# Sliding-window attention: for one head of four, the mask of the transposed scores is added by VectorE in PSUM instead of by a TensorE product

## The chip, the cores and the metric

One core of a Trainium2 chip runs the whole kernel. The metric is the device time of one execution in microseconds (us). A core has TensorE (PE; its weight loads are listed as PEld), VectorE (DVE), ScalarE (ACT), GpSimd (POOL) and SyncE (SP, which here only issues transfers). The engines run side by side, each through its own queue in order, and wait for each other by semaphores.

## The reference

The kernel computes a block with conditioning, sliding-window attention and an MLP over 2048 rows of 576 values, in float32. The change lies in attention alone:

```python
B, S, D = x.shape
H = 32; Dh = D // H; W = 256
q, k, v = ...                          # from x @ wqkv, 32 heads of 18
scores = jnp.einsum("bhqd,bhkd->bhqk", q, k) * (Dh ** -0.5)
idx = jnp.arange(S)
mask = (idx[:, None] - idx[None, :] >= 0) & (idx[:, None] - idx[None, :] < W)
scores = jnp.where(mask[None, None], scores, -1e9)
p = _softmax(scores, axis=-1)
o = jnp.einsum("bhqk,bhkd->bhqd", p, v)
```

Around it: a layer norm with scale and shift from a condition vector, the projection to q, k and v before, the output projection `wo` after, then a shifted token-mixing MLP (w1, w2) and a large channel MLP (w3, w4).

## The kernel before

The program has three phases. Phase A makes layer norm, q, k and v, attention and the output projection; phase B the token-mixing MLP; phase C the channel MLP. Each phase lists its steps with a time written by hand, and plays them in the order of these times. In phase A the queues of PE, GpSimd and SP follow that order as it is written; for DVE and ACT a scheduler sets the order from its own estimates of readiness.

Attention goes in 32 units. A unit is four heads (chunk `c` of 8 heads, half `hq`) and one group `g` of 512 query rows, in the order c, g, hq. Each unit passes two stages:

- `s2`, the row maxima. For 4 query blocks and 4 heads, PE writes scores `sc` (queries on partitions, up to 384 keys) to one of three PSUM banks (L477), and DVE adds a mask and takes the maximum of each row in one instruction (L484, with a short read of its accumulator). The negative maxima (`mr`, L490 and L491) are transposed on PE (`mT`), copied by ACT (`ms`) and written by a transfer into two rows of the unit's operand `U`, so that the second stage's product subtracts the maximum by itself.
- `s3`, the probabilities. For each key-block position `b` (order 0, 3, 1, 2; the first row group has no 0) and each head `q` from 0 to 3, PE writes a transposed score block `X` (keys on partitions, 384 columns of queries) to one of three PSUM banks (L526: one product for b = 1 and 2, two for 0 and 3), adds the mask with a product of an identity matrix and a bfloat16 mask over the 256 columns at both ends (L527), and ACT takes the exponential into `P` (L533). After the blocks 0 and 3, and again after 1 and 2, PE multiplies `P` with V (`av`, L548): for each head its own 32 columns of the array. ACT copies `av` out (L553), PE transposes it (`oT`), and DVE divides by the sums (L562, L566).

`s3` of one unit is woven with `s2` of the one or two units that follow it: on PE a product `sc` and a block `X` alternate. The eight PSUM banks are three for `sc`, three for `X`, one for transposes and one for `av`. A block `X` can only be written when the exponential three blocks earlier has freed its bank; an `sc` only when the maximum three earlier has.

Of the kernel before, what the change touches and what calls it, by code (L numbers as in the profile page):

```python
# [12 lines left out]
ALU = mybir.AluOpType  # L13
# [6 lines left out]
P = 128  # L20
# [30 lines left out]
class Kern:  # L51
# [75 lines left out]
    def phase_a(self):  # L127
        nc = self.nc
# [10 lines left out]
        with ExitStack() as st:  # L139
# [301 lines left out]
            def unit(c, g, hq):  # L441
                return units[(2 * g + hq) % 4]
# [62 lines left out]
            def s3(c, g, hq):  # L505
                QZ, KZ = unit(c, g, hq)
                Pb, Xb, abox = {}, {}, []
                banks = [0, 3, 1, 2] if g else [3, 1, 2]

                def sc(b, q):  # L510
                    def f():
                        if q == 0:
                            Pb[b] = pp.tile([P, 4, 3 * P], F32, tag="P", name=f"P{c}_{g}_{hq}_{b}", bufs=self.b_p)
                        j = q // 2
                        X = self.ps.tile([P, 3, P], F32, tag="st", name=f"X{c}_{g}_{hq}_{b}_{q}", bufs=self.b_st)
                        if b == 0:
                            mms = [(0, 1, 0, 0), (1, 2, 1, 0)]
                            mk = maskb[:, 1, :].unsqueeze(1).to_broadcast([P, 2, P])
                        elif b < 3:
                            mms = [(0, 3, b + 1, b - 1)]  # L520
                            mk = maskb
                        else:
                            mms = [(0, 2, 4, 2), (2, 1, 5, 3)]
                            mk = maskb[:, 0, :].unsqueeze(1).to_broadcast([P, 2, P])
                        for n, (x0, nb, kb, qb) in enumerate(mms):
                            nc.tensor.matmul(X[:, x0:x0 + nb, :].rearrange("p a b -> p (a b)"), KZ[:, j, kb * P:(kb + 1) * P], QZ[:, q, qb * P:(qb + nb) * P], start=(n == 0), stop=False)  # L526
                        nc.tensor.matmul(X[:, 0::2, :], self.identb, mk, start=False, stop=True)  # L527
                        Xb[b, q] = X
                    return f

                def expo(b, q):
                    def f():
                        nc.scalar.activation(Pb[b][:, q, :], Xb[b, q].rearrange("p a b -> p (a b)"), AF.Exp, scale=SCALE)  # L533
                    return f

                def av(b):
                    def f():
                        if not abox:
                            abox.append(self.ps.tile([P, 512], F32, tag="av", name=f"av{c}_{g}_{hq}", bufs=self.b_av))
                        first = b == banks[0]  # L540
                        segs = {0: [(-1, 0, 2 * P, P), (-2, 0, P, 0)],
                                1: [(0, 0, 3 * P, 0)] if g else [(0, 0, 2 * P, 0), (0, 2 * P, P, 2 * P)],
                                2: [(1, P, 3 * P, 0)],
                                3: [(2, 2 * P, 2 * P, 0), (3, 3 * P, P, 2 * P)]}[b]
                        for n, (kb, q0, w, p0) in enumerate(segs):
                            for q in range(4):
                                hv = (8 * c + 4 * hq + q) * VA
                                nc.tensor.matmul(abox[0][32 * q:32 * q + 32, q0:q0 + w], V[4 * g + kb][:, hv:hv + 32], Pb[b][:, q, p0:p0 + w], start=(first and n == 0), stop=(b == banks[-1]))  # L548
                    return f

                def fin1():
                    avs = pp.tile([P, 512], F32, tag="avs", name=f"avs{c}_{g}_{hq}", bufs=1)
                    nc.scalar.copy(avs, abox[0])  # L553
                    abox.append(avs)

                def fin2():
                    avs = abox[1]
                    pt = self.ps.tile([P, 4, 4, 32], F32, tag="tr", name=f"oT{c}_{g}_{hq}", bufs=1)
                    for i in range(4):
                        nc.tensor.transpose(pt[:, i].rearrange("p a b -> p (a b)"), avs[:, i * P:(i + 1) * P], self.ident)  # L560
                    rc = sm.tile([P, 4, 4], F32, tag="rc", name=f"rc{c}_{g}_{hq}", bufs=2)
                    nc.vector.reciprocal(rc, pt[:, :, :, DH])  # L562
                    if hq == 0:
                        orow[c, g] = pp.tile([P, 4, 144], F32, tag="o", name=f"o{c}_{g}", bufs=self.b_o)
                    o = orow[c, g]
                    nc.vector.tensor_tensor(out=o[:, :, hq * 72:hq * 72 + 72].rearrange("p t (h d) -> p t h d", d=DH), in0=pt[:, :, :, 0:DH], in1=rc.unsqueeze(3).to_broadcast([P, 4, 4, DH]), op=ALU.mult)  # L566

                def fin3():
                    if hq == 1:
                        nc.sync.dma_start(self.od[g].rearrange("(t p) d -> p t d", p=P)[:, :, c * 144:(c + 1) * 144], orow[c, g])  # L570

                steps = []
                n = 0
                for k, b in enumerate(banks):
                    for q in range(4):
                        steps += [(n, sc(b, q)), (n + self.l_e, expo(b, q))]
                        n += 1
                    if (len(banks) - k) % 2:
                        for b2 in banks[max(0, k - 1):k + 1]:
                            steps.append((n + self.l_av + (1 if k < len(banks) - 1 else 0), av(b2)))  # L580
                return steps, n, fin1, fin2, fin3
# [118 lines left out]
            for c in range(NCH):  # L700
                for g in range(NGA):
                    for hq in range(2):
                        tb = 2 * u + hq + shift
                        n = 2 * u + hq
# [480 lines left out]
    c_w, c_t = 8.1, 8.6  # L1185
    lt, l_e, l_av, l_f, l_o = 1.2, 0.1, 0.0, 0.1, 0.12
    l_m = 0.1
    m_s4 = "v"
    m_eng = "vv" + "m" * 14
    n_warm = (16,)  # L1190
# [31 lines left out]
```

## Time and profile before

| | |
|---|---|
| median of 3 runs (lowest to highest) | 1789.46 us (1785.65 to 1795.23) |
| the profiled execution: time | 1788.75 us |
| the profiled execution: span in the trace | 1786.9 us |
| PE busy, share of the span | 97% |
| DVE busy | 55% |
| ACT busy | 33% |
| GpSimd busy | 22% |

In the profile a group of instructions reads: line, engine, operation, output<-inputs, shape, count | busy us in all, mean ns of one | idle time of the engine just before them, and what ended it. Rows of the timeline read: start in us from the span's start, duration in us, engine, line, operation, with neighbours of one kind merged ("x4") and, in brackets, the engine's idle time before it and what ended that. Rows of waits read: who <- whom, us in total, times, the longest. A stretch of the span reads: its bounds, its length, then for PE, PEld, DVE, ACT and POOL the busy us and count, then the granted clock of TensorE, the share of the transfer engines and GB/s. The ends of matmuls are modelled in the trace, so neighbouring matmuls can overlap in the rows; starts are the surer numbers.

Attention's maxima begin at about 196 us and its last exponentials are at 657 us. Before lie the projections, from 660 to about 860 us phase B, then phase C to the end.

### The profile page before, as it was taken

The page shows a single profiled execution, that of the slowest core. Times are in us where ns is not written, and L with a number is a line of the kernel's source. Part 1 is how long each engine was busy: PE and PEld are TensorE (multiplying, and loading weights), DVE is VectorE, ACT ScalarE, POOL GpSimd, SP SyncE. Part 2 cuts the span into 40 slices and gives each one's busy share as a digit, 9 for nine tenths or more (in the row PEclk, how much of TensorE's full clock was granted, in tenths as well). Part 3 has the DMA queues.
Part 4 walks back from the last instruction along what each step waited for, and adds up shares of the span by engine and source line. Part 5 has one row for each costly group of instructions (what it writes and reads, how often), then busy time and mean ns, then how long its engine had stood idle before and what let it go on. Part 6 is the DMA issues. An engine that isn't in the chain of part 4 may idle for free.

```text
span 1786.9 us, 30143 instructions
## 1 busy us (share of the span) xinstructions
PE 1731.2 (97%) x11700; PEld 1501.8 (84%) x11700; DVE 977.6 (55%) x2674; ACT 594.5 (33%) x1262; POOL 390.1 (22%) x379
## 2 busy tenths in 40 slices
PE   7999999999998988999899999999999999999999
PEld 5898767677767768899799999999999999999998
DVE  5402387778777875877544444444444444444434
ACT  4622166666664444354211111111111111111111
POOL 5511102222030110201432333234421121122100
PEclk8999999999999997999999999999999999999999
DMA  6434544544444556632211111111110000000002
GB/s 178 122 101 155 181 124 134 136 118 140 119 139 126 172 176 190 202 101 78 86 48 35 42 55 40 36 49 55 55 35 16 29 26 16 29 29 29 1 1 106
DMA packets 97712, 156.88 MB, mean 88 GB/s; under 512 B 11035, under 2 KB 40479, under 8 KB 97571
## 3 DMA queue, kind: packets, MB, share of 16 engines
q1 hardware_dynamic: 86612, 135.12, 25.5%
q10 hardware_dynamic: 10958, 19.85, 3.1%
q8 instruction: 92, 1.51, 0.4%
q14 instruction: 50, 0.40, 0.1%
HBM read 107.06 MB, written 47.20 MB: 86 GB/s over the span
## 4 chain that ended last, share of the span: by engine, by line
PE 55%; DVE 2%; POOL 0%; issue 0%; DMA 0%; ACT 0%; SPq 0%; POOLq 0%; ACTq 0%; DVEq 0%
PE p L1147 26%; PE p L1118 22%; PE p L1120 2%; PE p L1119 2%; PE w L1012 2%; PE pg L959 2%; DVE x L1013 0%; DMA r<-in_B_w_dram 0%; DVE G L977 0%; POOL CW L1102 0%; DVE LNT L70 0%; DVE CW L1097 0%; DVE xm L886 0%; DVE G L964 0%; DVE Gc L1129 0%
## 5 line engine op out<-in xcount | busy, mean ns | idle before, releaser
L1147 PEld LDWEIGHTS p<-CW,Gc 128*128 128x128 f32 x3456 | 473.8, 188 | 16.2 <-DVE Gc L1129 3.7
L1147 PE MATMUL p<-CW,Gc 128*128 128x288 f32 x3456 | 482.0, 295 | 3.5 <-DVE Gc L1129 3.5
L1118 PE MATMUL p<-LNT,CW 128*128 128x512 f32 x1728 | 419.1, 391 | 0.0
L1118 PEld LDWEIGHTS p<-LNT,CW 128*128 128x128 f32 x1728 | 316.2, 188 | 58.8
L1126 ACT ACTIVATE gfc<-p 128x512 f32<-128x512 f32 x144 | 86.2, 599 | 735.5 <-PE p L1120 735.5
L1151 DVE TENSOR_TENSOR acc<-p,acc 128x288 f32<-128x288 f32 x340 | 153.8, 455 | 319.2 <-PE p L1147 315.9
L484 DVE CUSTOM_DVE_ANT_0 sc<-sc,mask 128x384 f32<-128x384 f32 (+2 forms) x512 | 261.8, 555 | 84.1 <-PE sc L477 81.3
L533 ACT ACTIVATE P<-X 128x384 f32<-128x384 f32 x480 | 221.8, 490 | 107.9 <-PE X L527 94.5
L477 PE MATMUL sc<-U 126*128 126x384 f32 (+2 forms) x512 | 197.8, 404 | 5.5 <-DVE m L484 3.9
L526 PE MATMUL X<-U 128*128 128x384 f32 (+2 forms) x704 | 181.9, 317 | 4.8 <-DMA U<-ms 1.9
L1151 DVE TENSOR_TENSOR accw<-p,accw 128x288 f32<-128x288 f32 x204 | 90.0, 453 | 129.5 <-PE p L1147 128.1
L526 PEld LDWEIGHTS X<-U 128*128 128x128 f32 x704 | 126.7, 191 | 35.3 <-issue 23.9
L527 PE MATMUL X<-maskb,identb 128*128 128x256 bf16 x480 | 136.1, 284 | 0.0
L1129 DVE TENSOR_TENSOR Gc<-gfc,Gc 128x512 fp32r<-128x512 f32 x144 | 124.8, 867 | 4.5
L422 PE MATMUL pq<-hT,Wq 128*128 128x512 f32 x504 | 122.0, 400 | 2.3 <-POOL Wq L380 1.6
L422 PEld LDWEIGHTS pq<-hT,Wq 128*128 128x128 f32 x504 | 95.0, 190 | 24.8 <-POOL Wq L380 1.9
L477 PEld LDWEIGHTS sc<-U 126*128 126x128 f32 x512 | 98.5, 197 | 13.4 <-DVE m L484 9.6
L1098 POOL TENSOR_TENSOR CW<-r,CW 128x1024 fp32r<-128x1024 f32 x17 | 41.5, 2440 | 283.2 <-DVE CW L1096 283.2
L548 PE MATMUL av<-P,V 128*32 128x256 f32 (+2 forms) x1472 | 91.0, 379 | 0.0
L1128 ACT CAST Gc<-gfc 128x512 fp32r<-128x512 f32 x144 | 89.4, 621 | 4.6
L1102 POOL TENSOR_TENSOR CW<-r,CW 128x1152 fp32r<-128x1152 f32 x17 | 46.4, 2728 | 158.3 <-DVE CW L1101 158.3
L527 PEld LDWEIGHTS <-identb 128*128 128x128 bf16 x480 | 46.0, 96 | 36.0 <-issue 18.6
(1056 smaller groups left out, 1973.5 us busy)
## 6 DMA issues: line engine op xcount, KB each, us to landing
U<-qkh SPq DMA_DIRECT2D x156, 72.0 KB
U<-qkh SPq DMA_DIRECT2D x96, 108.0 KB
r<-in_B_w_dram SPq DMA_DIRECT2D x18, 576.0 KB
qkh<-hl ACTq DMA_DIRECT2D x36, 256.0 KB
qkl<-hl ACTq DMA_DIRECT2D x36, 256.0 KB
r<-in_B_w_dram SPq DMA_DIRECT2D x18, 512.0 KB
U<-qkl SPq DMA_DIRECT2D x78, 72.0 KB
U<-qkl SPq DMA_DIRECT2D x48, 108.0 KB
```

Source lines behind the costliest of these rows:

```text
L422: nc.tensor.matmul(pq, a, b, start=(n == 0), stop=(n == len(pl) - 1))
L477: nc.tensor.matmul(sc[:, lo:], QZ[:KR, q, i * P:(i + 1) * P], KZ[:KR, j, i * P + lo:(i + 3) * P], start=True, stop=True)
L484: nc.vector.tensor_tensor_reduce(out=sc[:, lo:], in0=sc[:, lo:], in1=mask[:, lo:], scale=1.0, scalar=-3e38, op0=ALU.add, op1=ALU.max, accu ...
L526: nc.tensor.matmul(X[:, x0:x0 + nb, :].rearrange("p a b -> p (a b)"), KZ[:, j, kb * P:(kb + 1) * P], QZ[:, q, qb * P:(qb + nb) * P], start ...
L527: nc.tensor.matmul(X[:, 0::2, :], self.identb, mk, start=False, stop=True)
L533: nc.scalar.activation(Pb[b][:, q, :], Xb[b, q].rearrange("p a b -> p (a b)"), AF.Exp, scale=SCALE)
L548: nc.tensor.matmul(abox[0][32 * q:32 * q + 32, q0:q0 + w], V[4 * g + kb][:, hv:hv + 32], Pb[b][:, q, p0:p0 + w], start=(first and n == 0), ...
L1118: nc.tensor.matmul(pg, W3[:, ws, fs], L[:, xs, :], start=(i == 0), stop=False)
L1128: nc.scalar.copy(Gh, gf)
L1129: nc.vector.tensor_tensor(out=Gl, in0=gf, in1=Gh.bitcast(F32), op=ALU.subtract)
L1147: nc.tensor.matmul(po, a, w, start=(i == 0), stop=(i == len(seq) - 1))
L1151: nc.vector.tensor_tensor(out=acc[t][:, cs], in0=po, in1=acc[t][:, cs], op=ALU.add)
```

## The change

For head q = 3 of each four, the product that adds the mask is left out, the last product of the scores closes the accumulation, and DVE adds the same bfloat16 mask to the 256 end columns of `X` in place in PSUM. Each unit has 3 or 4 such blocks (b values), 120 in all. Heads 0 to 2 keep the mask product.

```diff
                         for n, (x0, nb, kb, qb) in enumerate(mms):
-                            nc.tensor.matmul(X[:, x0:x0 + nb, :].rearrange("p a b -> p (a b)"), KZ[:, j, kb * P:(kb + 1) * P], QZ[:, q, qb * P:(qb + nb) * P], start=(n == 0), stop=False)
-                        nc.tensor.matmul(X[:, 0::2, :], self.identb, mk, start=False, stop=True)
+                            nc.tensor.matmul(X[:, x0:x0 + nb, :].rearrange("p a b -> p (a b)"), KZ[:, j, kb * P:(kb + 1) * P], QZ[:, q, qb * P:(qb + nb) * P], start=(n == 0), stop=(q in self.q_dve and n == len(mms) - 1))
+                        if q in self.q_dve:
+                            nc.vector.tensor_tensor(out=X[:, 0::2, :], in0=X[:, 0::2, :], in1=mk, op=ALU.add)
+                        else:
+                            nc.tensor.matmul(X[:, 0::2, :], self.identb, mk, start=False, stop=True)
                         Xb[b, q] = X
...
     l_m = 0.1
+    q_dve = (3,)
     m_s4 = "v"
```

The added lines move those behind by three: ACT's exponential is L536 in the changed kernel, `av` L551, the copy of `av` L556; the mask product is L530 and the add L528.

PE's order in attention is the same but for the products that are gone, and those of GpSimd and SP are the same there. The places of the adds on DVE are the scheduler's. In the rows below the numbers of a name are group, half, block or query block, and head, then a running number. First DVE's queue in the block that ends unit (c=1, g=1, hq=1): the add of b = 1, head 3, while the maxima are already those of unit (g=2, hq=1).

```order
 L484 ISA sc_2_1_0_3_4267,m_2_1_4220<-sc_2_1_0_3_4267,mask 128x384
 L484 ISA m_2_1_4220 128x1
+L528 TENSOR_TENSOR X_1_1_1_3_4269<-X_1_1_1_3_4269,maskb 128x2x128
 L484 ISA sc_2_1_1_0_4274,m_2_1_4220<-sc_2_1_1_0_4274,mask 128x384
 L484 ISA m_2_1_4220 128x1
```

The add stands behind the maximum of the second query block of this stretch, and four maxima (heads 0 to 3 of query block 1) follow. Then, on the same queue, the add of b = 2, head 3, the unit's last block:

```order
 L484 ISA sc_2_1_1_3_4298,m_2_1_4220<-sc_2_1_1_3_4298,mask 128x384
 L484 ISA m_2_1_4220 128x1
+L528 TENSOR_TENSOR X_1_1_2_3_4301<-X_1_1_2_3_4301,maskb 128x2x128
 L484 ISA sc_2_1_2_0_4305,m_2_1_4220<-sc_2_1_2_0_4305,mask 128x384
 L484 ISA m_2_1_4220 128x1
```

It stands behind those four maxima and ahead of one more. PE goes on to `av` right after writing this block and the scores of that last maximum. On ACT, at the blocks 0 and 3 of the next unit (g=2, hq=0), the order was

```order
L533 ACTIVATE P_2_0_3_4373<-X_2_0_3_0_4374 128x384
L533 ACTIVATE P_2_0_3_4373<-X_2_0_3_1_4383 128x384
L533 ACTIVATE P_2_0_3_4373<-X_2_0_3_2_4392 128x384
L533 ACTIVATE P_2_0_3_4373<-X_2_0_3_3_4400 128x384
L533 ACTIVATE P_2_0_1_4406<-X_2_0_1_0_4407 128x384
```

and in the changed kernel, at the same place on ACT, it is

```order
L536 ACTIVATE P_2_0_3_4373<-X_2_0_3_0_4374 128x384
L536 ACTIVATE P_2_0_3_4373<-X_2_0_3_1_4383 128x384
L536 ACTIVATE P_2_0_3_4373<-X_2_0_3_2_4392 128x384
L536 ACTIVATE P_2_0_1_4406<-X_2_0_1_0_4407 128x384
L536 ACTIVATE P_2_0_3_4373<-X_2_0_3_3_4400 128x384
```

The exponential of block 3, head 3, has moved behind that of block 1, head 0. On DVE the add of that block 3, head 3, stands behind the last maximum of unit (g=2, hq=1) and just ahead of the two steps that make the negative maxima:

```order
 L484 ISA sc_2_1_3_3_4397,m_2_1_4220<-sc_2_1_3_3_4397,mask 128x384
 L484 ISA m_2_1_4220 128x1
+L528 TENSOR_TENSOR X_2_0_3_3_4400<-X_2_0_3_3_4400,maskb 128x2x128
 L490 TENSOR_SCALAR mr_2_1_4414<-m_2_1_4220 128x4x4
 L491 SCALAR_TENSOR_TENSOR mr_2_1_4414<-m_2_1_4220,mr_2_1_4414 128x4x4
```

Nothing else there has changed its place on DVE, except that the division (L566) can swap with a neighbouring maximum.

## The prediction

> **What bounds the kernel now.** I read the page's engine totals, then the busy time by stage, then the groups by line and shape, then the waits, and last the timeline of one attention unit.
>
> ```profile
> span 1786.9 us, 30143 instructions
> PE 1731.2 (97%) x11700; PEld 1501.8 (84%) x11700; DVE 977.6 (55%) x2674; ACT 594.5 (33%) x1262; POOL 390.1 (22%) x379
> ...
> 240.00:600.00 360.00, 346.65 (x3124) 255.84 (x3124) 281.19 (x1054) 221.38 (x484) 59.80 (x63) 1.00 0.47 132
> ```
>
> TensorE (PE) is the bound overall. The last row is the stretch in which nearly all of the changed work lies; after its length come PE, weight loads, VectorE (DVE), ScalarE (ACT), GpSimd. PE is busy 346.65 of 360 us (96%), DVE 281.19 (78%). So PE bounds this stage too, but DVE is a good second here, not the idle 55% of the page.
>
> ```profile
> L484 DVE CUSTOM_DVE_ANT_0 sc<-sc,mask 128x384 f32<-128x384 f32 x448 | 239.4, 581 | 60.1 <-PE sc L477 58.1
> L533 ACT ACTIVATE P<-X 128x384 f32<-128x384 f32 x480 | 221.8, 490 | 107.9 <-PE X L527 94.5 <-PE sc L477 7.8 <-DMA qkh<-hl 2.3
> L1151 DVE TENSOR_TENSOR acc<-p,acc 128x288 f32<-128x288 f32 x340 | 153.8, 455 | 319.2 <-PE p L1147 315.9
> L527 PE MATMUL X<-maskb,identb 128*128 128x256 bf16 x480 | 136.1, 284 | 0.0
> ...
> ACT P L533 <- PE X L527: 94.5, 113, 2.7
> ...
> PEld sc L477 <- DVE m L484: 9.6, 21, 1.3
> ```
>
> DVE's main work is the row maximum of the scores (L484); PE hardly waits for it (9.6 us in all), and ACT waits for PE. The 480 mask products (L527) are what the change touches: 120 of them, head q=3 of each four.
>
> **One unit.** X is a block of transposed scores, named b (key block) and q (head). The rows below are the part b1q3 to b2q3 of one unit, the products with V (`av`) that end it, and the start of the next.
>
> ```profile
> 360.23 0.44 PE L526 MATMUL X<-U 128*128 128x384 f32 x1
> ...
> 361.57 0.34 PE L526 MATMUL X<-U 128*128 128x384 f32 x1
> ...
> 361.75 0.28 PE L527 MATMUL X<-maskb,identb 128*128 128x256 bf16 x1
> 361.77 0.57 DVE L484 CUSTOM_DVE_ANT_0 sc<-sc,mask 128x384 f32<-128x384 f32 x1
> 361.79 0.42 PE L477 MATMUL sc<-U 126*128 126x384 f32 x1
> 362.05 0.34 PE L526 MATMUL X<-U 128*128 128x384 f32 x1
> 362.16 0.48 ACT L533 ACTIVATE P<-X 128x384 f32<-128x384 f32 x1
> ...
> 362.25 0.60 DVE L484 CUSTOM_DVE_ANT_0 sc<-sc,mask 128x384 f32<-128x384 f32 x1
> ...
> 362.77 0.60 DVE L484 CUSTOM_DVE_ANT_0 sc<-sc,mask 128x384 f32<-128x384 f32 x1
> 362.95 1.64 ACT L533 ACTIVATE P<-X 128x384 f32<-128x384 f32 x4 [0.32 <-PE sc L477]
> ...
> 363.29 0.60 DVE L484 CUSTOM_DVE_ANT_0 sc<-sc,mask 128x384 f32<-128x384 f32 x1
> 363.50 0.43 PE L526 MATMUL X<-U 128*128 128x384 f32 x1
> ...
> 363.80 0.60 DVE L484 CUSTOM_DVE_ANT_0 sc<-sc,mask 128x384 f32<-128x384 f32 x1
> ...
> 364.16 1.50 PE L548 MATMUL av<-P,V 128*32 128x384 f32 x16
> 364.31 0.60 DVE L484 CUSTOM_DVE_ANT_0 sc<-sc,mask 128x384 f32<-128x384 f32 x1
> ...
> 365.59 0.49 PE L526 MATMUL X<-U 128*128 128x128 f32 x2
> 365.80 0.59 ACT L553 COPY avs<-av 128x512 f32<-128x512 f32 x1 [1.22 <-PE av L548]
> ...
> 366.42 0.57 DVE L484 CUSTOM_DVE_ANT_0 sc<-sc,mask 128x384 f32<-128x384 f32 x1 [1.45 <-PE sc L477]
> ```
>
> DVE runs the maxima back to back, one every 0.515 us (362.77, 363.29, 363.80, 364.31), and only rests 1.45 us while PE does `av`. ACT finishes the last exponential of the unit at 362.95+1.64 = 364.59, inside the `av` that began at 364.16, so PE never waits for it.
>
> **What is removed.** From X b1q3 (361.57) to the next X (362.05) PE takes 0.48 us for 384+256+384 = 1024 columns, so a mask product of 256 columns is worth 0.48*256/1024 = 0.12 us. As a lower end stands the 0.04 us from its start to that of the next product (361.75 to 361.79). 120 of them give 4.8 to 14.4 us of PE. I take 0.12, since PE streams without gaps here. Their weight loads lie beside other products and count nothing.
>
> **What is added.** 120 adds of 128x256 on DVE. The nearest row is L1151, an add with a PSUM operand, 128x288 in 0.455 us; by its elements 0.404. I take 0.42 from start to end. For how long an add holds the next instruction off, two adds of that size and their successor stand here:
>
> ```profile
> 849.74 0.81 DVE L1013 TENSOR_TENSOR x<-w,x 128x288 f32<-128x288 f32 x2
> ...
> 850.47 0.45 DVE L85 BATCH_NORM_STATS2 d13st<-x 128x6 f32<-128x288 f32 x1
> ```
>
> (850.47-849.74)/2 = 0.365 us for 288 elements; I take 0.35 for 256. That is 42 us of DVE in all, on an engine with 360-281 = 79 us free in this stage. By capacity it fits; by place it may not, because DVE's free time lies behind the maxima, and the add of the block's last head stands behind them too.
>
> **The end of the first block.** By DVE's order the add of b1q3 stands behind the maximum that starts at 361.77, and four maxima stand between it and the add of b2q3. The first add takes the slot of 362.25 and passes DVE on at 362.60. Four maxima of 0.515 follow, to 364.66. The add of b2q3 runs 364.66 to 365.08. Its exponential takes 0.49 (L533), with about 0.04 us of hand-over on either side (a `sc` product's end to its maximum's start, below): 365.65. Only then can `av` do its last quarter, head q=3 of b2. The `av` has two sets (b1, b2) in 365.59-364.16 = 1.43 us, 0.71 each, and its four heads run side by side, so a late fourth head costs a set of its own: the next X starts at 365.65+0.71 = 366.36 and not at 365.59. Loss: 0.77 us, the saving of two products already lost in it. PE's inputs come in time for this: X b2q3 (363.50) is over a microsecond ahead of its add. Queued behind that add on DVE is one maximum alone, which the rest of 1.45 us covers; queued behind the late exponential on ACT is the copy of `av`, which waits for `av` anyway.
>
> **The end of the second block**, b0 and b3 of the next unit:
>
> ```profile
> 365.96 0.42 PE L477 MATMUL sc<-U 126*128 126x384 f32 x1
> ...
> 367.48 0.57 DVE L484 CUSTOM_DVE_ANT_0 sc<-sc,mask 128x384 f32<-128x384 f32 x1
> ...
> 368.02 0.57 DVE L484 CUSTOM_DVE_ANT_0 sc<-sc,mask 128x384 f32<-128x384 f32 x1
> ...
> 370.16 0.60 DVE L484 CUSTOM_DVE_ANT_0 sc<-sc,mask 128x384 f32<-128x384 f32 x1
> ...
> 370.79 1.51 PE L548 MATMUL av<-P,V 128*32 128x256 f32 x32
> 370.85 0.17 DVE L490 TENSOR_SCALAR mr<-m 128x16 fp32r<-128x16 f32 x1
> ...
> 372.23 0.44 PE L526 MATMUL X<-U 128*128 128x384 f32 x1
> ```
>
> (Hand-over: 365.96+0.42 = 366.38, the maximum starts at 366.42.) The add of b0q3 takes the slot of 368.02 and moves the rest by 0.35, so the last maximum, at 370.16 before, starts at 370.51 and the add of b3q3 behind it at 371.03, to 371.45. Exponential and hand-overs: 372.02. The `av` here has four sets in 372.23-370.79 = 1.44 us, b0 and b3 with 256 and 128 columns each, 0.72 per block. Head 3 of b3 thus ends at 372.02+0.72 = 372.74 and not 372.23. Loss: 0.51 us. The maxima's last step (370.85) comes 0.7 us later, and the transposes that use it stand in the next block, beyond.
>
> A unit of 12.0 us (X b1q1 at 360.23 to its like at 372.23) so grows by 0.77+0.51 = 1.28 us. PE has DVE's 1.45 us of rest again at each block's start, so the delay does not pile up over units.
>
> **The sum.** There are 32 units (L553 copies once for each). I count 16 like the one walked, with 4 adds and full-width maxima, at 1.25: 20 us. Another 11, which have 3 adds (first row group) or the short maxima of a first row group on DVE (64 of 512 are narrower than 384), I put at 0.8: 8.8 us. The last five are stretched by other PE work (output projection); estimate 0.4 each: 2 us. Together +31 us against this execution's own 1788.75: 1819.6. The median of the runs (1789.46) is 0.7 above, so 1820. What follows attention I let shift as it is: PE's longest wait there for a transfer is for attention's own output, which comes later too.
>
> ```profile
> PE oTT11pa L68 <- DMA or<-od: 5.6, 1, 5.6
> ```
>
> Bounds per unit: if a late fourth head costs only its wait and not a set of its own, +0.4 (27 units: +11 us, 1800); if X's three PSUM banks stall PE as well at b0q3 and b1q3 by about 0.4, +1.7 (+46, 1835, with the last five 1838).
>
> **Rivals.** *PE alone decides (faster).* If the scheduler's order leaves the fourth heads early enough, or PE has other work to do while they are late, PE keeps 120*0.12 = 14.4 us: 1774. For it speaks that PE waits only 9.6 us for DVE today; against it that PE's queue is in order and `av` directly follows the block's last X. It decides if the add of b2q3 ends before about 364.3, that is, if it is served ahead of at least two of the four maxima. The Trainium skill (Perfetto Trace Analysis, Identifying the Most-Contended Engine) says to optimize the engine with the highest occupancy first, which here is PE and gives this rival's time. The trace agrees that PE is that engine (96% of the stage) and leaves open whether the work taken off it returns as a wait.
>
> *A draw.* The two ends of blocks of 27 units lose 0.25 us each, 54*0.25 = 13.5 us, as much as PE gains: 1788. It needs adds of a fraction of 0.42 us, which no row supports.
>
> *DVE becomes the bound everywhere.* Each add costs its whole 0.42 us on PE, or X's banks stall it throughout: 120*0.42 = 50 us or more, 1839 and up. For it: with the adds DVE has 281+42 = 323 of 360 us; against it the rests of 1.45 us, in which it catches up.
>
> **How the numbers follow.** About 0.5%, 9 us, is what this kernel's measurement tells from no change. Forecast (1800 to 1838) 0.68; DVE-bound beyond that 0.12; draw 0.10; faster 0.10. The range 1797 to 1842 takes in the forecast, half of the DVE-bound case and the upper edge of the draw: about 0.8. Slower is 0.68+0.12 = 0.80.
>
> **What would show it.** Right: the distance of `av` copies in steady units grows from 12.0 to 13.2 us; the wait of `av` for the exponentials, nearly nothing before, becomes one of the longest of PE, some 0.4 to 0.8 us at each block's end; PE's share of this stage falls to about 90%; DVE's work there grows by about 40 us; an add takes 0.40 to 0.46 us. Wrong: adds much shorter or longer than that; PE waiting at X's banks rather than at `av`; unchanged unit lengths, which would say that the fourth head's set does overlap.

## The result

| | before | after |
|---|---|---|
| median (lowest to highest), 4 runs each beside each other | 1791.17 us (1785.65 to 1795.23) | 1830.26 us (1828.86 to 1832.28) |
| ratio, 95% interval | | 1.0224 [1.0209, 1.0238] |
| the profiled execution: time, span | 1788.75, 1786.9 us | 1832.28, 1830.5 us |

The change made the kernel 39 us slower; the forecast was 1820 (1797 to 1842). The page of the changed kernel and the stretch from 240 to 600 us (after its length: PE, PEld, DVE, ACT, POOL, then granted clock, share of the transfer engines, GB/s):

```profile
span 1830.5 us, 30098 instructions
...
PE 1759.4 (96%) x11580; PEld 1506.6 (82%) x11580; DVE 1015.9 (55%) x2794; ACT 592.6 (32%) x1262; POOL 390.4 (21%) x379
...
240.00:600.00 360.00, 339.68 (x2826) 235.92 (x2825) 288.02 (x1082) 207.99 (x457) 56.51 (x55) 1.00 0.44 120
```

PE runs 120 products fewer and is listed as busy 28 us longer (1759.4 against 1731.2). That is no more work. The groups of `av` at 384 columns show where it comes from, first before, then after:

```profile
L548 PE MATMUL av<-P,V 128*32 128x384 f32 x448 | 42.6, 491 | 0.0
```

```profile
L551 PE MATMUL av<-P,V 128*32 128x384 f32 x448 | 60.0, 493 | 3.7 <-ACT P L536 3.7
```

The products are as many and as long (491 and 493 ns), but cover 60.0 us instead of 42.6: the four heads of a set used to overlap in the array, and now the fourth runs by itself. All widths of `av` together cover 119.1 us on the page of the changed kernel and 91.0 on that of before. So a part of the loss hides as busy PE. The weight loads' share of a stretch gives it away: in the one above PEld went from 255.84 to 235.92 us. Their sum over the whole execution does not, it rose from 1501.8 to 1506.6 us with 120 loads fewer, since the late head's loads overlap less as well (those of `av` cover 48.7 us instead of 42.3).

The time in stretches, bounded by the copies of `av` (L553, now L556), from the two profiles:

| us | before | after | difference | forecast |
|---|---|---|---|---|
| to the first unit's copy | 235.0 | 236.8 | +1.8 | in the next row |
| 26 steps from unit to unit | 310.4 | 338.9 | +28.5 | 28.8 |
| the last five units | 112.8 | 122.0 | +9.2 | 2 |
| after attention | 1128.7 | 1132.8 | +4.1 | 0 |

The waits that grew, by who waits, for whom, us in total, times, the longest:

```profile
ACT P L536 <- DVE X L528: 74.9, 90, 4.2
...
PEld av L551 <- ACT P L536: 26.5, 51, 2.1
PEld X L526 <- ACT P L536: 18.8, 29, 0.9
PEld sc L477 <- DVE m L484: 17.6, 45, 1.6
```

Three places pay: `av` at the ends of blocks (0.4 us in all before), X at its PSUM banks (4.1 before) and `sc` at its own (9.6 before). One steady unit of the changed kernel, from its blocks 0 and 3 to its end, in the timeline:

```profile
380.43 0.50 PE L526 MATMUL X<-U 128*128 128x128 f32 x2
...
385.66 0.46 DVE L528 TENSOR_TENSOR X<-X,maskb 128x256 f32<-128x256 f32 x1
385.71 1.82 PE L551 MATMUL av<-P,V 128*32 128x256 f32 x32
386.15 0.49 ACT L536 ACTIVATE P<-X 128x384 f32<-128x384 f32 x1 [0.37 <-DVE X L528]
...
387.47 0.45 PE L526 MATMUL X<-U 128*128 128x384 f32 x1
...
389.50 0.47 DVE L528 TENSOR_TENSOR X<-X,maskb 128x256 f32<-128x256 f32 x1
...
390.74 0.44 PE L526 MATMUL X<-U 128*128 128x384 f32 x1 [0.44 <-ACT P L536]
...
391.75 2.12 PE L551 MATMUL av<-P,V 128*32 128x384 f32 x16
391.99 0.47 DVE L528 TENSOR_TENSOR X<-X,maskb 128x256 f32<-128x256 f32 x1
...
392.49 0.49 ACT L536 ACTIVATE P<-X 128x384 f32<-128x384 f32 x1 [0.66 <-DVE X L528]
...
393.80 0.49 PE L526 MATMUL X<-U 128*128 128x128 f32 x2
```

Blocks 0 and 3 take 387.47-380.43 = 7.04 us (before 372.23-365.59 = 6.64), blocks 1 and 2 take 393.80-387.47 = 6.33 (before 365.59-360.23 = 5.36). The unit is 13.37 us instead of 12.0. At 391.99 the add of b2q3 starts when `av` has begun already; its exponential ends at 392.49+0.49 = 392.98, and the next X stands 0.82 us behind that. At 390.74 stands a second stall: X of b2q2 needs the bank of b1q3, three blocks back, whose exponential had to wait for the add of 389.50.

### The profile page after: what moved, and what is told of

Read it like the earlier page. It is cut to its first block, busy times and chain, and to the rows that moved or that the text cites. A ratio compares the mean times of both kernels' runs of the same rounds, so it can differ in the third digit from the quotient of the medians.

```text
span 1830.5 us, 30098 instructions
## 1 busy us (share of the span) xinstructions
PE 1759.4 (96%) x11580; PEld 1506.6 (82%) x11580; DVE 1015.9 (55%) x2794; ACT 592.6 (32%) x1262; POOL 390.4 (21%) x379
## 4 chain that ended last, share of the span: by engine, by line
PE 72%; DVE 7%; ACT 2%; DMA 2%; issue 1%; ACTq 1%; SPq 0%; POOL 0%; DVEq 0%; POOLq 0%
PE p L1150 25%; PE p L1121 21%; PE av L551 5%; PE X L526 4%; PE sc L477 3%; PE pg L962 3%; PE w L1015 2%; PE po L766 2%; PE p L1123 2%; PE p L1122 2%; DVE sc L484 2%; PE X L530 1%; ACT P L536 1%; DMA hbd<-xr 1%; ACTq L501 1%
## 5 line engine op out<-in xcount | busy, mean ns | idle before, releaser
L536 ACT ACTIVATE P<-X 128x384 f32<-128x384 f32 x480 | 217.3, 491 | 161.9 <-PE X L530 76.3
L477 PE MATMUL sc<-U 126*128 126x384 f32 (+2 forms) x512 | 192.3, 392 | 8.8 <-DVE m L484 6.4
L526 PEld LDWEIGHTS X<-U 128*128 128x128 f32 x704 | 123.5, 190 | 46.2 <-ACT P L536 18.8
L551 PE MATMUL av<-P,V 128*32 128x256 f32 (+2 forms) x1472 | 119.1, 380 | 6.4 <-ACT P L536 6.3
L477 PEld LDWEIGHTS sc<-U 126*128 126x128 f32 x512 | 97.5, 194 | 21.9 <-DVE m L484 17.6
L530 PE MATMUL X<-maskb,identb 128*128 128x256 bf16 x360 | 101.9, 283 | 0.0
L551 PEld LDWEIGHTS av<-P,V 128*32 128x32 f32 x1472 | 48.7, 109 | 58.7 <-ACT P L536 26.5
```

Source lines behind the costliest of these rows:

```text
L477: nc.tensor.matmul(sc[:, lo:], QZ[:KR, q, i * P:(i + 1) * P], KZ[:KR, j, i * P + lo:(i + 3) * P], start=True, stop=True)
```

## The experiments

The theory: an add costs nothing by itself; it makes one exponential late, and PE's queue in order pays where that exponential is the next thing it needs. Rivals: VectorE's load costs wherever the adds stand; and the product taken off PE is a gain of 14.4 us that hides in the sum. The first two experiments look at the gain and the load by themselves.

**No product and no add.** Head 3 of each four goes without a mask, and its exponential has the scale 0, so that its values stay harmless.

```diff
-nc.vector.tensor_tensor(out=X[:, 0::2, :], in0=X[:, 0::2, :], in1=mk, op=ALU.add)
+pass
...
-... AF.Exp, scale=SCALE)
+... AF.Exp, scale=0.0 if q in self.q_dve else SCALE)
```

> Head 3 has no mask product and no add (its scores stay unmasked; its exponential is taken of 0, so that nothing overflows). It prices the 120 products that are removed. Theory (PE streams without gaps, 0.12 us a product): 14.4 us less than before, 1775. If a product is only worth the 0.04 us between its start and the next: 5 us less, 1785.

Measured: 1785.17 us (1783.74 to 1789.67), ratio 0.998 [0.9969, 0.999]. Without anything in its place the removal is worth 3.6 us [1.8, 5.5], 0.03 us a product, near the lower end. Where the rest goes stands in the pair of blocks 1 and 2; ACT's issue of the transfer of `ms`, the exponentials behind it and X of b2q3 before, and then, from X of b1q3 on, without the mask:

```profile
374.29 0.62 ACTq L501 DMA_DIRECT2D U<-ms  x1
...
374.95 1.64 ACT L533 ACTIVATE P<-X 128x384 f32<-128x384 f32 x4 [0.31 <-PE sc L477]
...
375.50 0.45 PE L526 MATMUL X<-U 128*128 128x384 f32 x1
```

```profile
372.33 0.34 PE L526 MATMUL X<-U 128*128 128x384 f32 x1
...
372.68 0.34 PE L526 MATMUL X<-U 128*128 128x384 f32 x1
...
373.04 0.62 ACTq L501 DMA_DIRECT2D U<-ms  x1
...
373.70 1.64 ACT L536 ACTIVATE P<-X 128x384 f32<-128x384 f32 x4 [0.32 <-PE X L530]
...
374.25 0.19 PEld L526 LDWEIGHTS X<-U 128*128 128x128 f32 x1 [0.23 <-ACT P L536]
```

From X to X PE does save 372.68-372.33 = 0.35 against 0.48 us: the 0.12 us of the prediction are there. But X of b2q3 needs the bank of b2q0. The exponential of b2q0 is the first of the four, and it starts right behind the issue of the transfer in ACT's queue: 0.04 us behind it both times (374.29+0.62 = 374.91, then 374.95; 373.04+0.62 = 373.66, then 373.70). X of b2q3 follows 0.55 us later both times. So what PE saves at b1q3 it waits for at b2q3. In the whole kernel the waits of X for exponentials rose from 4.1 to 8.3 us and those of `sc` for maxima from 9.6 to 12.6, without any add.

**The load without the late exponential.** As above, and DVE makes 128 adds of up to 256 columns on the `sc` banks, after each fourth head's maximum. The probabilities don't wait for them, but they stand in DVE's queue ahead of later maxima, and each works on an `sc` bank.

```diff
+if q in self.q_dve:
+    e = sc[:, max(lo, P):]
+    nc.vector.tensor_tensor(out=e, in0=e, in1=mask[:, max(lo, P):], op=ALU.add)
```

> As the run without mask products for head 3, and DVE makes 128 adds (112 of 128x256, 16 of 128x128) on score banks after their maximum, in PSUM, four in a unit: the same work on DVE in nearly the same places, but no exponential waits for it, only the score bank. Theory (the loss is the late exponential of the fourth head ahead of av): most of the gain stays, 1775 to 1785. Rival (DVE's load itself, or score banks that come free late): near the changed kernel, 1815 to 1830.

Measured: 1802.29 us (1800.39 to 1805.55), ratio 1.0069 [1.0048, 1.0091], between the two: 17 us over the kernel without adds. The waits of `sc`, first those that ended with a maximum, then those that ended with one of the adds:

```profile
PEld sc L477 <- DVE m L484: 26.7, 65, 1.8
...
PEld sc L477 <- DVE sc L487: 2.5, 4, 0.7
```

Without adds the first was 12.6. So the load isn't free, although no probability waits for it: the trace puts most of these waits down to maxima, which come later with an add ahead of them in the queue, and few to a bank that an add still holds. This run doesn't separate the two, since its adds did both; so the rival that VectorE's load has a price of its own stands where PE is close to waiting for maxima.

**Adds only where a block ends** (b = 2 and 3; the product elsewhere), **and only in the middle** (b = 0 and 1). The edit of the first; the second has `(0, 1)`:

```diff
-if q in self.q_dve:
+if q in self.q_dve and b in (2, 3):
     nc.vector.tensor_tensor(out=X[:, 0::2, :], ...)
```

> The add on DVE only in the blocks b=2 and b=3 (64 of the 120), the mask product kept in b=0 and b=1. In b=2, and in b=3 of all units, the fourth head is the last block ahead of av. Theory: nearly all of the loss, 1815 to 1828 (a little of PE's gain is missing, and a little of DVE's delay). Rival (load on DVE): half of the loss, about 1809.

> The reverse: the add on DVE only in b=0 and b=1 (56 of the 120), where another block follows before av. Theory: PE's gain of 56*0.12 = 7 us, less small stalls at X's banks: 1782 to 1793. Rival (load on DVE): half of the loss, about 1808.

Measured: 1815.05 us (1814.18 to 1815.76), ratio 1.0139 [1.0121, 1.0156], for the ends, and 1810.6 (1807.1 to 1812.28), 1.0111 [1.009, 1.0132], for the middles. The first lies at the lower edge of what the theory expected, the second misses the theory's 1782 to 1793 by far. In the profiles the 26 steps grow by 15.6 and 12.5 us; their sum, 28.1, is nearly the 28.5 of the full change, but partly by chance: of the 12.5 us 3.9 are one step, in which PE waited 1.92 us for a transfer and the granted clock fell to 0.57 for 4 us:

```profile
346.00:350.00 4.00, 4.00 (x20) 3.68 (x21) 2.29 (x8) 1.52 (x4) 0.00 (x0) 0.57 0.48 111
```

The surer evidence is the ordinary full unit: there the adds at the ends cost 0.5 to 0.8 us, those in the middles about 0.5, and the full change 1.0 to 1.4. So there are two losses, and they add. A part of the 21 us of the middles may be the clock's: these four executions had a mean granted clock of 0.985 to 0.986, those of the kernel before 0.988 to 0.991. The ends:

```profile
PEld av L551 <- ACT P L536: 22.5, 39, 2.2
```

```profile
366.99 0.44 PE L526 MATMUL X<-U 128*128 128x384 f32 x1
...
370.80 2.15 PE L551 MATMUL av<-P,V 128*32 128x384 f32 x16
...
371.58 0.49 ACT L536 ACTIVATE P<-X 128x384 f32<-128x384 f32 x1 [0.61 <-DVE X L528]
...
372.89 0.49 PE L526 MATMUL X<-U 128*128 128x128 f32 x2
```

Blocks 1 and 2 take 5.90 us instead of 5.36; from the start of `av` to the next X it is 2.09 us, not 1.43. The last exponential ends at 372.07, and 0.82 us follow: a set of its own for the late head. The middles have hardly a wait of `av`, but this one (and 17.6 us of `sc` for maxima, the longest 3.9):

```profile
PEld X L526 <- ACT P L536: 18.1, 28, 0.9
```

**One middle at a time.** Of the 120 adds 64 stand at ends, 32 at b1, and 24 at b0 (the first row group has no b0; the expectations below say 32). Both are the first block of their pair, but behind b0q3 PE has the four transposes of the unit before, and its blocks 0 and 3 take two products each, so that it comes later to the bank.

```diff
-if q in self.q_dve and b in (0, 1):
+if q in self.q_dve and b == 1:     # and in the other kernel b == 0
```

> The add for the fourth head of query block b1 alone (32 of 128; the first block of its pair), the product everywhere else. In the kernel with the adds of b0 and b1 the wait of X of b2, third head, on the exponential of b1, fourth head, lasted 0.45 us in a unit, and the pair b1/b2 took 5.85 us against 5.36. Theory that this add costs by the bank of X that it holds: that pair is 0.4 to 0.5 us longer in each of 25 units, the pair b0/b3 unchanged, the waits of X for exponentials near 18 us as there, and the time 1800 to 1806. Rival that the two kinds of first block share the loss, by VectorE's load: about half of the 20 us of that kernel, 1798 to 1801, with the pair only 0.2 us longer and waits of X near 9 us.

> The add for the fourth head of query block b0 alone (32 of 128). Its exponential is followed by those of four pairs of b3 before X or av waits for it, so by the theory that an add costs only where its exponential is waited for, the time is that of before, 1787 to 1792, the unit 12.0 us. Rival that VectorE's load costs wherever the add stands (96 of the maxima behind it come 0.37 us later): 1794 to 1800, with more waits of sc for maxima than the 9.6 us of before.

Measured: 1801.37 us (1800.19 to 1808.32), ratio 1.0069 [1.0044, 1.0095], for b1, and 1791.24 (1787.89 to 1795.82), 0.9999 [0.9986, 1.0012], for b0. Both as the theory had it. The waits of b1 alone, and its pair of blocks 1 and 2:

```profile
PEld X L526 <- ACT P L536: 17.0, 26, 0.9
```

```profile
376.06 0.44 PE L526 MATMUL X<-U 128*128 128x384 f32 x1
...
379.32 0.44 PE L526 MATMUL X<-U 128*128 128x384 f32 x1 [0.44 <-ACT P L536]
...
381.90 0.49 PE L526 MATMUL X<-U 128*128 128x128 f32 x2
```

The pair takes 5.84 us, 0.48 longer, in 25 units some 12 us; its median is 9 us above that of before. With b0 alone a unit stays at 12.0 to 12.1 us and nothing is lost, with the same add in the same queue. So 24 adds cost nothing measurable at a place where nobody waits for them. `sc` does wait 12.7 us for maxima, more than the 9.6 of before, as the rival had it; but that is no more than the 12.6 of the run without any add. That a load of 120 adds would cost nothing by itself is not shown. Nothing is gained by b0 either. Its unit shows why; before, and then with b0 alone, X of b1q0, two scores, `av`:

```profile
381.96 0.42 PE L526 MATMUL X<-U 128*128 128x384 f32 x1
...
382.26 0.63 PE L477 MATMUL sc<-U 126*128 126x384 f32 x2
...
382.83 1.51 PE L548 MATMUL av<-P,V 128*32 128x256 f32 x32
```

```profile
369.00 0.42 PE L526 MATMUL X<-U 128*128 128x384 f32 x1
...
369.39 0.72 PE L477 MATMUL sc<-U 126*128 126x384 f32 x2
...
370.03 1.51 PE L551 MATMUL av<-P,V 128*32 128x256 f32 x32
```

From X to `av` it is 1.03 us instead of 0.87. The 0.12 us that PE saved at b0q3 is given back 2 us later, between that X and `av`.

**The last five units alone** have the adds:

```diff
-if q in self.q_dve:
+if q in self.q_dve and (c, g, hq) > (3, 1, 0):
```

> The add on DVE only in the last five units, those that the output projection stretches; the mask product kept in the other 27. The prediction put them at +2 us; by the trace of the changed kernel the stretch of the last five grew by 9.3 us. If that is theirs alone: 1798 to 1800. If it is carried over from the units before: 1789 to 1792.

Measured: 1801.75 us (1800.62 to 1804.15), ratio 1.0066 [1.0045, 1.0087], a little above the 1798 to 1800 expected. In the profile these five units take 121.8 us against 112.8. So the 9 us are theirs. The longest waits of an exponential for an add stand there, and one of them reads:

```profile
572.94 0.34 PE L526 MATMUL X<-U 128*128 128x384 f32 x1
...
574.40 0.58 DVE L889 TENSOR_SCALAR xr<-xr,c0mv,c0rs 128x576 f32<-128x576 f32 x1 [1.01 <-POOL c0rs L89]
574.90 0.45 DVE L767 TENSOR_TENSOR xr<-po,xr 128x288 f32<-128x288 f32 x1
575.26 0.42 DVE L528 TENSOR_TENSOR X<-X,maskb 128x256 f32<-128x256 f32 x1
...
575.72 0.49 ACT L536 ACTIVATE P<-X 128x384 f32<-128x384 f32 x1 [4.15 <-DVE X L528]
...
576.26 0.14 PEld L551 LDWEIGHTS av<-P,V 128*32 128x32 f32 x2 [2.08 <-ACT P L536]
```

X was written by 573.28. The add came at 575.26, because DVE's queue stood 1.01 us at a layer norm step that waits for GpSimd, and then did that step and a residual add. `av` stood 2.08 us. In these units DVE has the output projection's residual and norms to do as well, and the add inherits their waits.

**Head 0 instead of head 3** takes the add as far from `av` as a block allows:

```diff
-q_dve = (3,)
+q_dve = (0,)
```

> The add on DVE for head 0 in place of head 3, the same number of adds and products. Theory: head 0 is three blocks ahead of av, so its add and exponential are done in time, and what is left is PE's gain of 14 us less stalls at X's banks: 1778 to 1800. Rival (load on DVE): as the changed kernel, about 1830.

Measured: 1807.11 us (1805.6 to 1809.87), ratio 1.0096 [1.0074, 1.0118]: less than half of the loss stays, but the time is above the theory's 1800, and the 26 steps keep 15.7 of their 28.5 us. The wait of `av` is nearly gone (2.3 us), the one at X's banks remains:

```profile
PEld X L526 <- ACT P L536: 14.3, 42, 0.7
```

**`av` one block later.** In the table of times `av` is put behind one more X of the next block, once with the adds and once, as its control, without:

```diff
-lt, l_e, l_av, l_f, l_o = 1.2, 0.1, 0.0, 0.1, 0.12
+lt, l_e, l_av, l_f, l_o = 1.2, 0.1, 1.0, 0.1, 0.12
```

> The changed kernel with l_av = 1, so that av stands one block X and one score product later in PE's queue in most places. Theory: the fourth head's exponential has some 0.5 us more at most block ends, and a good part of the loss goes: 1800 to 1815. Rival (load on DVE): no change, about 1830.

> The control of the run with av later: the kernel before (mask products for all heads) with l_av = 1. PE does not wait for exponentials there, so both theories expect no change: 1785 to 1795.

Measured: 1832.15 us (1827.02 to 1834.0), ratio 1.0224 [1.0195, 1.0253], with the adds, and 1819.8 (1813.51 to 1825.42), 1.0164 [1.0132, 1.0196], without. The control was expected not to move and lost 30 us: so arranged, X waits for its banks without any add. That wait is less than half of the 30 us; the rest was not followed up, and a part may be the clock's (the mean granted clock was 0.981 to 0.987 in these two kernels and 0.986 to 0.990 before). Between the two lie 12 us instead of 39, and `av` no longer waits for exponentials; the wait is X's now (first with the adds, then without):

```profile
PEld X L526 <- ACT P L536: 33.1, 51, 2.0
```

```profile
PEld X L526 <- ACT P L536: 17.0, 29, 1.0
```

The loss at the ends can be taken away, but this way costs as much as it brings. An add served earlier in DVE's queue, ahead of the maxima, was not tried. No version here is measurably faster than before and still masks every head.

## Why the prediction held, and where its terms were off

- **Where the loss comes from: right.** "Only then can `av` do its last quarter": the late fourth head costs a set of its own, 0.82 us from its exponential to the next X where 0.71 was forecast. The wait of `av` for exponentials went from 0.4 to 26.5 us, one of PE's longest, as announced.
- **The unit: 13.37 us measured, 13.28 forecast, but split otherwise.** The end of the first block lost 0.97 us (forecast 0.77), that of the second 0.40 (0.51). The first holds two losses: 0.54 at `av` (the run with adds at the ends) and 0.48 at X's banks (the run with b1). The working left the second to its upper bound, "if X's three PSUM banks stall PE as well at b0q3 and b1q3 by about 0.4". It happens at b1q3 and not at b0q3, while `av` lost 0.23 less than walked at the first block and the second block 0.11 less. So the unit was right partly by luck, because these errors met.
- **The 27 steady units:** 30.3 us (1.8+28.5) against 28.8. By the copies of `av` the full units grew by 1.2 us on average and the reduced ones by 1.0, against the estimates of 1.25 and 0.8. By the prediction's own rule 13 of these 27 are full and not 16: the other three lie among the last five.
- **The last five units: mis-sized, 9.2 us against 2.** That they are "stretched by other PE work" was taken as cover. It is the opposite: there DVE has other work too, and its queue in order puts waits of up to 1 us ahead of an add.
- **The price of the removed product:** 0.12 us of PE locally, as taken, but 0.03 us end to end. Taking the upper value did no harm, since the block ends were walked by times and not by the sum of prices. It did mislead the rivals: "PE alone decides" at 1774 could not be had even with adds for nothing; 1785 was the most.
- **The most-contended engine.** PE was the busiest engine, and taking 120 products off it gained 0.2%. The Trainium skill (Perfetto Trace Analysis, Identifying the Most-Contended Engine) says to optimize that engine first. The run without mask or add gives no more than that 0.2% for it here, because PE then waits more at its PSUM banks, X for exponentials and `sc` for maxima. The same section of the Trainium skill says that matmul busy time is no good measure of how close a kernel is to its limit, and names the weight loads' busy share, beside one other, as what to use instead. The trace agrees for the share: PE's busy time rose by 28 us on less work, while the weight loads' share of the stretch fell from 71 to 66% (the loads of the 120 products, at 96 ns each 11.5 us in all, are part of that). Their busy time in all rose by 4.8 us.
- **The signs.** "PE's share of this stage falls to about 90%" was wrong, since late products count as busy: it reads 94%. Of the signs of being wrong one came half true: PE waits at X's banks as well, 18.8 us beside the 26.5 at `av`.
- **After attention:** 0 forecast, 4.1 in the profile. The row below, of the changed kernel, shows a clock of 0.62 for 9 us, which is at most 3.4 us; the profile of before has its low clocks right behind attention, up to 760 us, and no other until its last microseconds. The run without mask or add has such a stretch too (0.62 from 863 to 872 us), and its remainder was 1127.7, so this alone doesn't settle it. With b0 alone and head 0 the remainder was 1128.6 and 1127.3, so it is not the adds' steady price. What set the clock back, and where the rest of the 4.1 us comes from, stays open.

```profile
911.00:920.00 9.00, 6.63 (x27) 6.15 (x28) 5.01 (x10) 0.93 (x3) 3.34 (x2) 0.62 0.34 98
```

- **The size of an add:** 0.452 us on average (forecast 0.42, announced 0.40 to 0.46); a slot of 0.37 where the next DVE instruction follows at once (0.35). DVE's busy time grew by 38.3 us (about 40).

```profile
L528 DVE TENSOR_TENSOR X<-X,maskb 128x256 f32<-128x256 f32 x120 | 54.2, 452 | 0.0
```

## What to carry to other kernels

Before moving a step to an engine with free time, ask for each place who needs the result next and how many steps stand between: here the same add cost nothing at b0, 0.48 us at b1 and 0.54 at the end of the first block. Price the removal by the pace of the loop it leaves, not by the instruction: a product that isn't the pacemaker gives its time back at the next bank. And where an engine in order takes other work, its waits become the moved step's own.

## What the runs showed of the hardware that was not expected

- Products for four heads in side-by-side columns overlap in the trace (448 of 491 ns cover 42.6 us); once one head is late it runs apart from the others, and PE's busy time for `av` rises by 28.1 us over all widths (91.0 to 119.1) with not one product more.
- What VectorE's adds cost goes by their place: 128 adds of up to 256 columns on `sc` banks, among the maxima, cost 17 us, though no probability waits for them, and 24 adds on banks that nobody waits for cost nothing (0.9999 [0.9986, 1.0012]). The counts differ, so this is no price per add.
- A product taken off the busiest engine can come back whole at the next PSUM bank: X of b2q3 started 0.55 us behind the exponentials with and without the product of b1q3, because these stood behind the issue of a transfer (0.62 us) in ACT's queue.
